# Attention and gated unit on one core: earlier first row maxima, and shorter GpSimd batches ahead of the routing pieces

## The chip, the core and the metric

The kernel runs on one core of a Trainium2 chip. The metric is the device time of one execution in microseconds (us). Before the change it is 1684.03 us, the median of three runs (1683.86, 1684.03 and 1685.21). Differences of under about 0.2% (3.4 us) are small beside what such runs tell apart; the text takes that as its bound for "no change".

The engines are named as in the profile: PE is TensorE (matmuls), PEld its weight loads, DVE is VectorE, ACT is ScalarE, POOL is GpSimd, SP is SyncE, which only issues DMAs here.

## The reference

Input x is 2048 tokens by 512. All arithmetic is in fp32.

```python
def _A_ref(x, wqkv, wo):                      # H = 32 heads, Dh = 16
    q, k, v = ...                             # x @ wqkv, split into heads
    p = softmax(einsum("bhqd,bhkd->bhqk", q, k) * Dh ** -0.5)
    return einsum("bhqk,bhkd->bhqd", p, v) ... @ wo

def _B_ref(x, w_gate, w_up, w_down):          # F = 1792
    return einsum("bsf,fd->bsd", sigmoid(x @ w_gate) * (x @ w_up), w_down)

g = sigmoid((x * gate_w).sum(-1, keepdims=True))
return g * _A_ref(x, ...) + (1 - g) * _B_ref(x, ...)
```

The sum `(x * gate_w).sum(-1)`, one number for each token, is what the text calls the routing logit.

## The kernel before

Every fp32 operand of the projections is held as a high and a low part (`xh`, `xl`), and a product is three matmuls (high by high, high by low, low by high). The softmax subtracts a row maximum, which has to be known before the exponentials of that row are made. So the scores are computed twice: once for the maxima (`sm_step`, line 292: a matmul into a PSUM bank, then a DVE reduction over it, line 294), and once, later and transposed, for the exponentials (`st_part`, line 679 and 681).

PE is used as two halves. A matmul with 64 rows or fewer takes the lower or the upper half of the array, and two such matmuls run side by side. Where a product has 128 rows, class `Sum` issues it as two halves, LOW and UP (line 162). Two Sums go together, one with its LOW halves while the other has its UP halves; then they change sides. The change of sides goes through a token: `turn` puts a no-operation on POOL that waits for the last matmul of the side, and the next half on PE waits for that no-operation (line 173 in the trace's lines). POOL's program is in order, so the token has its place behind the POOL work that was recorded ahead of it.

The order on PE, DVE, ACT and POOL is as the program records it. The order of the DMAs on SP is not written by hand; a scheduler places them.

The stages that the change touches are two.

**The value tiles.** After the first projections there are eight steps, t = 0, 2, ..., 14. In each, two Sums of 12 products (v for two blocks of 128 tokens) give 24 places, 12 for side LOW and 12 for side UP, each with one half of each Sum. Into these places go the first row maxima of the first pair of heads: 44 calls of `first_max`. One call is two matmuls into two of the four banks sm0 to sm3, one on each half of PE, and two DVE reductions. The tables `FIRST` and `EARLIEST` (the latter for t = 0) say at which place (side, 0 to 11) how many calls stand. A bank can be written again only when its reduction has read it. The maxima read `qs` and `ks`, which a DMA brings from DRAM.

**The periods.** Then come 256 periods, k = 0 to 255, each recorded by the string `STEADY`: eight maxima matmuls (m), eight score matmuls (t) and twelve dense halves (d) of a Sum that the generator `filling` hands out, one Sum a period, with the turn in the middle; then `values(k)`, sixteen short matmuls (line 842). The Sums of kind "side" come four to a job. Their weights are combined and split into high and low parts on POOL ("op", "hi", "lo" below: lines 448, 139 and 136), from two tiles that DMAs load.

POOL's work waits in queues (`later`, then `turnover`, then `slow`). `work(length)` takes steps from them until their estimated costs reach the length, and is called with 2.0 after the turn and with 2.6 at the period's end. When a job's last Sum is done, all steps of the next job's weights that are still in `turnover` are recorded at once (`while end in turnover`), at the end of that period, ahead of the next period's token.

In periods 75 to 122 six periods make a group, r = (k - 75) % 6. At r = 0 and 3 a DMA loads a tile "sq" (`split_load`), at r = 1 and 4 POOL splits it (`split_sum`, a cast and a subtraction), at r = 1 a DMA loads two blocks of x (`logit_load`), and at r = 3 and 4 DVE makes one block's logits each (`logits`: the multiplication with a sum, line 829). The tiles sq and x share two buffers, so some loads of sq wait for the second logits. Every eighth period DVE also ends a half of the maxima (lines 298 and 300, "mpad" and "mt"); its instructions stand at the start of the periods with k % 8 = 5.

Of the kernel before, what the change touches and what calls it, by code (L numbers as in the profile page):

```python
# [42 lines left out]
LOW, UP = 0, 1  # L43
# [3 lines left out]
def gated_mix(ctx, tc, x, xT, wqk, wv, wo, w_gate, w_up, w_down, gate_w, out):  # L47
# [8 lines left out]
    def turns(tiles):  # L56
        turn = iter(range(1 << 30))
        return lambda: tiles[next(turn) % len(tiles)]
# [112 lines left out]
    def turn(*runs):  # L171

        token = pool.nop()
        tc.add_manual_dep(token.ins, runs[-1].last.ins.name, SYNC, reason=SHARED)
        for r in runs:
            r.token = token
# [5 lines left out]
    def work(length):  # L182
        length -= over[0]
        while length > 0.3 and (later or turnover or slow):
            cost, step = (later or turnover or slow).pop(0)
            step()
            length -= cost
        over[0] = max(0.0, -length)
# [52 lines left out]
    def load_pair(p, cols=slice(0, S)):  # L241
        for t, src in enumerate((q_d, k_d)):
            for b in range(2):
                rows, r = slice((2 * p + b) * DH, (2 * p + b + 1) * DH), 64 * b
                to = (QS, KS)[t][p % 2]
                if t == 0:
                    two, one = src[:, rows, cols].rearrange("a d s -> d a s"), src[0, rows, cols]
                else:
                    two, one = src[0, rows, cols].unsqueeze(1), src[1, rows, cols]
                    two = two.to_broadcast([DH, 2, cols.stop - cols.start])  # L250
                sp.dma_start(to[r:r + 2 * DH, cols].bitcast(F32), two)
                sp.dma_start(to[r + 2 * DH:r + KM, cols].bitcast(F32), one)
# [50 lines left out]
    def put_max(half):  # L303

        p, i = half
        mt = mrow.pop(half)
        hl = keep.tile([P, 2, 32], F32R, name=f"mhl{p}_{i}", tag="mhl", bufs=2)

        def low():
            pool.tensor_tensor(hl[:, 1, :], mt, hl[:, 0, :].bitcast(F32), ALU.subtract)  # L310
            d = max_d[2 * p + i]
            sp.dma_start(d.rearrange("k r a j -> (k r) a j"), hl.bitcast(F32))
            for b in (1, 0):
                for a in range(2):
                    r = 64 * b + 3 * DH + a
                    rows_in[p, i] = sp.dma_start(QS[p % 2][r:r + 1, i * 1024:(i + 1) * 1024].rearrange(
                        "o (t k j) -> o t k j", t=8, k=4).bitcast(F32),
                        d[:, 8 * b:8 * b + 8, a, :].rearrange("k t j -> t k j").unsqueeze(0))
        return [(1.6, lambda: pool.tensor_copy(hl[:, 0, :], mt)), (0.25, low)]  # L319
# [293 lines left out]
    def first_max():  # L613
        if first:
            j, i = first.pop(0)
            one = sm_step(j)
            one(0, i)
            one(1, i)
# [36 lines left out]
    def tokens(t):  # L655
        return [((xh[:, k, t * P:(t + 1) * P], xl[:, k, t * P:(t + 1) * P]), w_v[k]) for k in range(KT)]

    def put_v(t, o, engine):
        to = v[:, t, :].rearrange("p (h c) -> p h c", c=VW)[:, :, :DH]
        o = o.rearrange("p (h c) -> p h c", c=DH)  # L660
        if engine is act:
            act.activation(to, o, AF.Copy)  # L662
        else:
            engine.tensor_copy(to, o)
# [3 lines left out]
    def st_part(k, b):  # L668

        p, r = divmod(2 * k, 32)  # L670
        i, kt = divmod(r, 16)
        qs, ks = QS[p % 2], KS[p % 2]
        r = 64 * b
        pt = ptile[k, b] = mid(f"p{k}_{b}")
        for a in range(2):
            for c in range(2):
                o = bank()
                q0 = i * 1024 + c * 512
                pe.matmul(o, ks[r:r + KR, (kt + a) * P:(kt + a + 1) * P], qs[r:r + KR, q0:q0 + 512],  # L679
                          start=True, stop=True)  # L680
                act.activation(pt[:, 2 * a + c, :], o, AF.Exp, scale=DH ** -0.5)  # L681
                yield

    FIRST = {(LOW, 2): 1, (LOW, 7): 1, (UP, 0): 2, (UP, 5): 1, (UP, 9): 1}
    EARLIEST = {(LOW, 10): 1, (UP, 0): 1, (UP, 4): 1, (UP, 9): 1}
    bank = turns([dn, banks[0]])
    ahead = st_part(0, 1)
    for t in range(0, NS, 2):
        two = [Sum(bankv(), tokens(t + a)) for a in range(2)]
        for g in (LOW, UP):  # L690
            for m in range(3 * KT):
                for _ in range((FIRST if t else EARLIEST).get((g, m), 0)):
                    first_max()
                two[0].half(g)
                two[1].half(1 - g)
                if (0, 0) in mrow and m == 2:
                    for _, step in put_max((0, 0)):
                        step()
                if t == NS - 2 and (g, m) in ((LOW, 11), (UP, 2), (UP, 5), (UP, 8)):
                    next(ahead)  # L700
                if t >= 12 and m == 6 and g == UP:
                    work(2.6)
            if g == LOW:
                turn(*two)
        if t < NS - 2:
            for a in range(2):
                put_v(t + a, two[a].o, act)
# [98 lines left out]
    def split_load(r):  # L806
        f, t, c = r // 8, r // 4 % 2, r % 4
        e = split_in[r] = keep.tile([P, 2, 512], F32R, name=f"sq{r}", tag="ev", bufs=2)
        sp.dma_start(e[:, 0, :].bitcast(F32), s_d[t, f, :, c * 512:(c + 1) * 512])

    def split_sum(r):
        f, t, c = r // 8, r // 4 % 2, r % 4
        e = split_in.pop(r)

        def store():
            for a in range(2):
                sp.dma_start((q_d, k_d)[t][a, (2 + f) * P:(3 + f) * P, c * 512:(c + 1) * 512],
                             e[:, 1 - a, :].bitcast(F32))
        split_later(e[:, 1, :], e[:, 0, :], e[:, 0, :].bitcast(F32), store)
# [3 lines left out]
    def logit_load(t):  # L823
        tok[t] = keep.tile([P, 2, D], F32, name=f"xn{t}", tag="ev", bufs=2)
        sp.dma_start(tok[t], x[t * P:(t + 2) * P, :].rearrange("(t p) d -> p t d", p=P))

    def logits(t, a):
        xn = tok[t][:, a, :]
        dve.tensor_tensor_reduce(xn, xn, gwb, scale=1.0, scalar=0.0, op0=ALU.mult, op1=ALU.add,
                                 accum_out=logit[:, t + a:t + a + 1])  # L830

    sums = {}

    def values(k):
# [67 lines left out]
    for k in range(NPER):  # L902
        n = 2 * k
        if n + LEAD == NSTEP:
            bank = bank7
            leave = dve.tensor_copy
        if 75 <= k < 123:
            t, r = divmod(k - 75, 6)
            if r in (0, 3):
                split_load(2 * t + r // 3)  # L910
            if r in (1, 4):
                split_sum(2 * t + r // 3)
            if r == 1:
                logit_load(2 * t)
            if r in (3, 4):
                logits(2 * t, r - 3)
        if n % 32 == 0 and n // 32 + 1 < NPAIR:
            load_pair(n // 32 + 1)
        parts["t0"], parts["t1"] = st_part(k, 0), st_part(k + 1, 1) if k + 1 < NPER else iter(())
        emit(STEADY if k < FREE else LAST, **parts)  # L920
        if run and run.done():
            run = next(fill, None)
        elif run and run.n:
            turn(run)
        for half in list(mrow):
            later[:0] = put_max(half)
        work(2.6)
        later.extend(soon)
        soon.clear()
        if k == NPER - 1:  # L930
            break
        if NPER - 16 < k <= NPER - 12:
            for _ in range(2):
                next(next(exps))
        spot[:] = [seven[SUMS]]
        values(k)
        if k == NPER - 17:
            loaded.extend(hidden_load(*chunks[m]) for m in range(2))
            early = [hidden_early(m) for m in range(2)]
            exps = iter([early[0]] * 4 + [early[1]] * 4)  # L940
        if 192 <= k < 215 and k % 8 != 4:
            next(dens[0], None)
        if k == NPER - 6:
            next(dens[1])
        if k == NPER - 2:
            raws = [late_raw(*late[m][:2]) for m in range(2)]
        if k == NPER - 13:
            early = chain(*early)
        if k >= NPER - 13:
            for _ in range(1 if k < FREE else 3):  # L950
                next(early, None)
# [137 lines left out]
```

## Time and profile before

| | |
|---|---|
| median of three runs | 1684.03 us |
| the profiled execution | 1684.2 us, of which the span from the first to the last instruction is 1682.4 us |
| PE busy in the span | 1677.3 us (100%) |
| DVE, ACT, POOL busy | 1451.8 us (86%), 1362.8 us (81%), 941.9 us (56%) |
| granted clock of TensorE | 1.000 |
| the value tiles | from 27.8 to 85.75 us |
| the periods 75 to 122 | about 503 to 771 us |

A row of the timeline gives the start in us, the duration in us, the engine, the line of the kernel, the operation, output<-inputs, the shapes and a count; in square brackets stands the time for which the engine had been idle before, and what ended that. Rows "SPq" are DMAs as SP issues them. PE's matmuls are pipelined, so that a duration of 0.39 us there does not mean that the next one waits so long. In a table by windows there stand, for a stretch, its length and each engine's busy time and instructions. Since PE is busy nearly all the time, the share of busy time tells little; what can be seen is whether the distance from one matmul to the next is longer than it is elsewhere.

### The profile page before, as it was taken

How to read it: one execution, taken by the hardware profiler on the slowest of the kernel's cores; microseconds unless marked ns; L12 is line 12 of the kernel's file. 1: busy time of each engine (PE TensorE's matmuls, PEld its weight loads, DVE VectorE, ACT ScalarE, POOL GpSimd, SP SyncE). 2: the span in 40 equal slices, each digit the busy share in tenths (PEclk: the TensorE clock that was granted, in tenths of full speed). 3: DMA queues.
4: the chain of work that ended last, by engine and by line, in shares of the span. 5: the costliest groups of instructions: out<-in, count | busy, mean ns of one | idle time of the engine just before them, and what ended most of it. 6: DMA issues, size and time to landing. Idle time of an engine off the chain costs nothing.

```text
span 1682.4 us, 34644 instructions
## 1 busy us (share of the span) xinstructions
PE 1677.3 (100%) x12485; PEld 1063.3 (63%) x12485; DVE 1451.8 (86%) x2347; ACT 1362.8 (81%) x2659; POOL 941.9 (56%) x922
## 2 busy tenths in 40 slices
PE   9999999999999999999999999999999999999999
PEld 7766566665656565656565666656565656568887
DVE  7988888888889999999888888888999888887853
ACT  4188898989888898889898989898898989983431
POOL 1034476547666666666666767676766667653110
PEclk9999999999999999999999999999999999999999
DMA  7511457356565564566635353534353534368861
GB/s 247 140 48 59 128 175 210 134 164 209 143 199 133 167 153 157 159 165 184 166 102 146 102 145 108 134 103 133 107 137 104 133 115 153 128 205 277 294 211 70
DMA packets 143788, 254.20 MB, mean 151 GB/s; under 512 B 24256, under 2 KB 36544, under 8 KB 140736
## 3 DMA queue, kind: packets, MB, share of 16 engines
q1 hardware_dynamic: 136000, 237.30, 47.1%
q10 hardware_dynamic: 7616, 14.68, 2.8%
q8 instruction: 98, 1.61, 0.4%
q14 instruction: 74, 0.61, 0.2%
HBM read 149.42 MB, written 102.50 MB: 150 GB/s over the span
## 4 chain that ended last, share of the span: by engine, by line
PE 97%; DVE 3%; issue 0%; DVEq 0%
PE dn L162 29%; PE sm L842 27%; PE sm L292 15%; PE sm L1034 5%; PE st L679 5%; PE sm L679 4%; PE st L292 2%; DVE stat L294 2%; PE dn L1034 2%; PE st L1034 2%; PE st L643 1%; PE st L149 1%; PE sm L149 1%; PE st L162 1%; PE st L842 1%; PE st L85 0%
## 5 line engine op out<-in xcount | busy, mean ns | idle before, releaser
L294 DVE TENSOR_REDUCE stat<-sm 128x1 f32<-128x512 f32 x1313 | 847.9, 681 | 140.4 <-PE sm L679 126.5
L681 ACT ACTIVATE p<-st 128x512 f32<-128x512 f32 x1019 | 619.2, 655 | 1.1 <-PE st L679 1.1
L681 ACT ACTIVATE p<-sm 128x512 f32<-128x512 f32 x1027 | 611.1, 632 | 0.5 <-PE sm L679 0.2
L292 PE MATMUL sm<-ks,qs 48*128 48x512 f32 x1313 | 522.6, 436 | 0.3
L842 PE MATMUL sm<-p,v 128*17 128x512 f32 x4016 | 480.0, 595 | 0.0
L294 DVE TENSOR_REDUCE stat<-st 128x1 f32<-128x512 f32 x735 | 479.5, 680 | 0.1
L679 PE MATMUL sm<-qs,ks 64*128 64x512 f32 x1027 | 427.6, 419 | 0.0
L679 PE MATMUL st<-qs,ks 64*128 64x512 f32 x1019 | 426.5, 419 | 0.0
L292 PEld LDWEIGHTS sm<-ks,qs 48*128 48x128 f32 x1313 | 239.6, 184 | 259.3 <-DVE stat L294 212.3
L859 POOL TENSOR_TENSOR sum<-sum,part 128x512 f32<-128x512 f32 x224 | 288.6, 1288 | 135.7 <-PE sm L679 118.4
L292 PE MATMUL st<-ks,qs 48*128 48x512 f32 x735 | 290.5, 395 | 0.0
L842 PEld LDWEIGHTS sm<-p,v 128*17 128x17 f32 x4016 | 93.2, 97 | 224.2 <-issue 155.1
L847 ACT ACTIVATE part<-sm 128x512 f32<-128x512 f32 x214 | 128.2, 599 | 124.4 <-issue 83.8
L542 POOL TENSOR_TENSOR chain<-chain,chain 128x512 f32<-128x512 f32 x96 | 124.1, 1292 | 156.3 <-PE sm L679 139.5
L679 PEld LDWEIGHTS st<-qs,ks 64*128 64x128 f32 x1019 | 187.7, 184 | 30.0 <-issue 3.4
L679 PEld LDWEIGHTS sm<-qs,ks 64*128 64x128 f32 x1027 | 189.6, 185 | 9.9 <-issue 5.1
L542 POOL TENSOR_TENSOR had<-chain,had 128x512 f32<-128x512 f32 x96 | 123.5, 1287 | 39.3 <-PE sm L679 20.3
L292 PEld LDWEIGHTS st<-ks,qs 48*128 48x128 f32 x735 | 137.3, 187 | 2.1 <-ACT v L662 0.3
L607 ACT ACTIVATE chain<-dn 128x512 f32<-128x512 f32 x128 | 89.2, 697 | 0.0
L542 POOL TENSOR_TENSOR side<-side,side 128x512 f32<-128x512 f32 x32 | 41.3, 1292 | 76.5 <-PE sm L679 66.1
L104 POOL TENSOR_TENSOR ol<-ot,oh 128x512 fp32r<-128x512 f32 (+1 forms) x8 | 14.7, 1840 | 102.5 <-ACT oh L101 102.5
L319 POOL CAST mhl<-mt 128x32 fp32r<-128x32 f32 x32 | 7.5, 236 | 102.7 <-DVE mt L300 102.7
(913 smaller groups left out, 3253.5 us busy)
## 6 DMA issues: line engine op xcount, KB each, us to landing
gul<-gu_d SPq DMA_DIRECT2D x56, 512.0 KB
had<-gu_d SPq DMA_DIRECT2D x84, 256.0 KB
gu_d<-had SPq DMA_DIRECT2D x84, 256.0 KB
gu_d<-side SPq DMA_DIRECT2D x56, 256.0 KB
pv_d<-sum SPq DMA_DIRECT2D x32, 256.0 KB
qs<-q_d SPq DMA_DIRECT2D x30, 256.0 KB
ks<-k_d SPq DMA_DIRECT2D x30, 256.0 KB
gu_d<-far SPq DMA_DIRECT2D x28, 256.0 KB
```

The costliest lines, as they stand in the source:

```text
L149: pe.matmul(o, a, b, start=(i == 0), stop=(i == len(ops) - 1))
L162: mm = pe.matmul(self.o, a[rows], b[rows], start=(self.n == 0), stop=(self.n == 2 * len(self.ops) - 1))
L292: pe.matmul(t, qs[r:r + KM, qt * P:(qt + 1) * P], ks[r:r + KM, g * 512:(g + 1) * 512], start=True, stop=True)
L294: dve.tensor_reduce(stat[half][:, b, qt % 8, g:g + 1], t, axis=AX.X, op=ALU.max)
L542: pool.tensor_tensor(to, u, w, ALU.add)
L607: leave = lambda e, o: act.activation(e, o, AF.Copy)
L679: pe.matmul(o, ks[r:r + KR, (kt + a) * P:(kt + a + 1) * P], qs[r:r + KR, q0:q0 + 512], start=True, stop=True)
L681: act.activation(pt[:, 2 * a + c, :], o, AF.Exp, scale=DH ** -0.5)
L842: pe.matmul(o[32 * c:32 * c + VW, :], v[:, 2 * k % 16 + a, h * VW:(h + 1) * VW], pts[c // 2][:, 2 * a + c % 2, :], start=(a == 0), stop=(a ...
L847: act.activation(e, o, AF.Copy)
L859: pool.tensor_tensor(s, s, e, ALU.add)
L1034: pe.matmul(down[t], a, b, start=(f == 0 and m == 0), stop=(f == NF - 2 and m == 5))
```

## The change

Three things change; what is computed stays the same.

First, the tables of the value tiles. At t = 0 there are now seven calls of `first_max` (from place LOW 1 on) where there were four (from LOW 10 on). At t = 2 and 4 there are six as before, one of them now at UP 10. From t = 6 on there are five in place of six. The last step, t = 14, has five in place of the four that were left over. The two calls in a row at the turn (UP 0) stay, and the call ahead of them moves from LOW 7 to LOW 8.

Second, the length of POOL's batch at the end of a period is 1.4 in place of 2.6 where the next period has logits.

Third, of the 16 logits pieces two, those of periods 85 and 109, are given in periods 86 and 110.

```diff
-    FIRST = {(LOW, 2): 1, (LOW, 7): 1, (UP, 0): 2, (UP, 5): 1, (UP, 9): 1}
-    EARLIEST = {(LOW, 10): 1, (UP, 0): 1, (UP, 4): 1, (UP, 9): 1}
+    FIRST = {(LOW, 3): 1, (LOW, 8): 1, (UP, 0): 2, (UP, 6): 1}
+    EARLIEST = {(LOW, 1): 1, (LOW, 4): 1, (LOW, 8): 1, (UP, 0): 2, (UP, 5): 1, (UP, 9): 1}
...
-                for _ in range((FIRST if t else EARLIEST).get((g, m), 0)):
+                for _ in range((FIRST if t else EARLIEST).get((g, m), 0) + (t in (2, 4) and (g, m) == (UP, 10))):
                     first_max()
...
+    def logits_at(k):
+        if not 75 <= k < 123:
+            return 0
+        r = (k - 75) % 6
+        return (r == 3) + 2 * (r == 4 and k % 8 != 5 or r == 5 and k % 8 == 6)
...
-            if r in (3, 4):
-                logits(2 * t, r - 3)
+            if logits_at(k):
+                logits(2 * t, logits_at(k) - 1)
...
-        work(2.6)
+        work(1.4 if logits_at(k + 1) else 2.6)
```

**PE at a turn of the value tiles.** The rows are PE's matmuls of step t = 6, from the last call ahead of the turn on. The lines 292 are a call's two matmuls (sm_69 to sm_72 are the four banks), the lines 162 are halves of the step's two Sums (st_66 and st_67). Before:

```order
L292 MATMUL sm_71<-ks_101,qs_100 128x512
L292 MATMUL sm_72<-ks_101,qs_100 128x512
L162 MATMUL st_66<-wv_l,xh 128x512
L162 MATMUL st_67<-wv_l,xh 128x512
L162 MATMUL st_66<-wv_h,xl 128x512
L162 MATMUL st_67<-wv_h,xl 128x512
L162 MATMUL st_66<-wv_h,xh 128x512
L162 MATMUL st_67<-wv_h,xh 128x512
L162 MATMUL st_66<-wv_l,xh 128x512
L162 MATMUL st_67<-wv_l,xh 128x512
L162 MATMUL st_66<-wv_h,xl 128x512
L162 MATMUL st_67<-wv_h,xl 128x512
```

Ten halves stand between this call and the turn's two calls, which come next. The same place now:

```order
L292 MATMUL sm_69<-ks_101,qs_100 128x512
L292 MATMUL sm_70<-ks_101,qs_100 128x512
L162 MATMUL st_66<-wv_h,xl 128x512
L162 MATMUL st_67<-wv_h,xl 128x512
L162 MATMUL st_66<-wv_h,xh 128x512
L162 MATMUL st_67<-wv_h,xh 128x512
L162 MATMUL st_66<-wv_l,xh 128x512
L162 MATMUL st_67<-wv_l,xh 128x512
L162 MATMUL st_66<-wv_h,xl 128x512
L162 MATMUL st_67<-wv_h,xl 128x512
L292 MATMUL sm_71<-ks_101,qs_100 128x512
L292 MATMUL sm_72<-ks_101,qs_100 128x512
```

Eight halves stand between this call and the first of the turn's two calls, which is the last two rows here. The turn's second call follows at once, on the banks that the first two rows of this fence write.

**POOL in the periods 77 to 79.** The rows are POOL's operations from the end of period 77 on. side_8r and side_1r are the raw weight tiles that DMAs load, side(0, 1)h and side(0, 1)l the high and low parts of the next job's weights (two blocks of each, one after the other), sq is the tile of `split_sum`; the lines 542 and 859 (865 now) are additions of the side Sums and of the value sums. Before:

```order
L448 TENSOR_TENSOR side_8r<-side_8r 128x256
L139 CAST side(0, 1)h<-side_8r 128x256
L136 TENSOR_TENSOR side(0, 1)l<-side_8r,side(0, 1)h 128x256
L542 TENSOR_TENSOR side_01_6288<-side_01_6288,side_00_6213 128x512
L859 TENSOR_TENSOR sum_1_5965<-sum_1_5965,part_6302 128x512
L448 TENSOR_TENSOR side_8r<-side_8r,side_1r 128x256
L448 TENSOR_TENSOR side_1r<-side_1r,side_8r 128x256
L139 CAST side(0, 1)h<-side_1r 128x256
L859 TENSOR_TENSOR sum_1_5965<-sum_1_5965,part_6371 128x512
L139 CAST sq_6304<-sq_6304 128x512
L136 TENSOR_TENSOR side(0, 1)l<-side_1r,side(0, 1)h 128x256
L136 TENSOR_TENSOR sq_6304<-sq_6304 128x512
```

Here the first three rows belong to the end of period 77, the two lines 448 and the cast after them to the end of 78, and only the last two rows to the end of 79. Now:

```order
L542 TENSOR_TENSOR side_01_6288<-side_01_6288,side_00_6213 128x512
L865 TENSOR_TENSOR sum_1_5965<-sum_1_5965,part_6299 128x512
L448 TENSOR_TENSOR side_8r<-side_8r 128x256
L865 TENSOR_TENSOR sum_1_5965<-sum_1_5965,part_6366 128x512
L139 CAST sq_6301<-sq_6301 128x512
L139 CAST side(0, 1)h<-side_8r 128x256
L136 TENSOR_TENSOR side(0, 1)l<-side_8r,side(0, 1)h 128x256
L448 TENSOR_TENSOR side_8r<-side_8r,side_1r 128x256
L448 TENSOR_TENSOR side_1r<-side_1r,side_8r 128x256
L139 CAST side(0, 1)h<-side_1r 128x256
L136 TENSOR_TENSOR side(0, 1)l<-side_1r,side(0, 1)h 128x256
L136 TENSOR_TENSOR sq_6301<-sq_6301 128x512
```

The seven rows from the cast "side(0, 1)h<-side_8r" on now all belong to the end of period 79, and so stand between the cast of sq and the token of period 80's turn. At the end of period 103 the same seven stand in place of the same two.

**DVE from the end of period 84 on.** The first two rows end a half of the maxima, the lines 829 are the second logits of the group (written as two instructions here, one in the trace), and the lines 294 are the reductions of the next maxima. Before:

```order
L298 TENSOR_REDUCE mpad_94<-stat_1_6236 128x16
L300 STREAM_TRANSPOSE mt_1_6769<-mpad_94 128x32
L829 ISA xn_6585,logit<-xn_6585,gwb 128x512
L829 ISA logit 128x1
L294 TENSOR_REDUCE stat_0_6798<-sm_72 128x1
```

Now:

```order
L298 TENSOR_REDUCE mpad_94<-stat_1_6236 128x16
L300 STREAM_TRANSPOSE mt_1_6769<-mpad_94 128x32
L294 TENSOR_REDUCE stat_0_6797<-sm_72 128x1
L294 TENSOR_REDUCE stat_0_6797<-st_65 128x1
L294 TENSOR_REDUCE stat_0_6797<-st_67 128x1
```

The logits follow now after the eighth of these reductions, one period later. At 109 it is the same.

## The prediction

> **What bounds the kernel now.** The page comes first, with the busy times and the shares of the chain of waits:
>
> ```profile
> PE 1677.3 (100%) x12485; PEld 1063.3 (63%) x12485; DVE 1451.8 (86%) x2347; ACT 1362.8 (81%) x2659; POOL 941.9 (56%) x922
> PE 97%; DVE 3%; issue 0%; DVEq 0%
> ```
>
> PE is the bound, and the change takes no matmul from it and adds none. So it can only move the gaps between matmuls. I read those in two places: the value tiles, where the first maxima move, and the periods 75 to 122. For the value tiles, this is the table by windows, one row a step from t = 0 to 14 (behind the busy time of each engine stand its instructions):
>
> ```profile
> core 0: us, PE busy (x) PEld busy (x) DVE busy (x) ACT busy (x) POOL busy (x), PEclk, DMA share, GB/s
> 27.80:34.55 6.75, 6.75 (x57) 5.36 (x58) 4.58 (x8) 0.60 (x1) 0.00 (x0) 1.00 0.97 242
> 34.55:41.55 7.00, 7.00 (x61) 5.46 (x59) 6.80 (x12) 1.09 (x2) 0.00 (x0) 1.00 0.51 155
> 41.55:48.90 7.35, 7.25 (x63) 6.09 (x61) 7.35 (x13) 1.08 (x2) 0.00 (x0) 1.00 1.03 253
> 48.90:56.05 7.15, 7.15 (x62) 5.69 (x60) 7.15 (x13) 1.08 (x2) 0.00 (x0) 1.00 1.06 217
> 56.05:63.25 7.20, 7.20 (x62) 5.65 (x60) 7.20 (x13) 1.08 (x2) 0.00 (x0) 1.00 0.98 313
> 63.25:70.45 7.20, 7.20 (x64) 5.78 (x62) 7.06 (x14) 1.09 (x2) 0.30 (x2) 1.00 0.06 24
> 70.45:78.20 7.75, 7.65 (x64) 5.87 (x62) 7.75 (x14) 1.09 (x2) 2.61 (x4) 1.00 0.09 24
> 78.20:85.75 7.55, 7.55 (x65) 6.25 (x61) 6.22 (x11) 3.38 (x6) 1.29 (x1) 1.00 0.07 19
> ```
>
> From t = 2 to t = 12 DVE is busy for the whole step: twelve reductions fill about 7.2 us. PE's gaps sit where it asks for a bank that DVE has not read yet. The timeline of the turn of t = 4:
>
> ```profile
> 44.33 0.39 PE L162 MATMUL st<-wv_h,xh 64*128 64x512 f32 x1
> 44.56 0.39 PE L162 MATMUL st<-wv_l,xh 64*128 64x512 f32 x1
> ...
> 45.53 0.18 PEld L292 LDWEIGHTS sm<-ks,qs 48*128 48x128 f32 x1 [0.41 <-DVE stat L294]
> 45.54 0.50 PE L162 MATMUL st<-wv_h,xh 64*128 64x512 f32 x1
> 45.87 0.40 PE L162 MATMUL dn<-wv_h,xh 64*128 64x512 f32 x1
> ```
>
> Two halves that run side by side, or the two matmuls of a call, take one slot: 44.56 - 44.33 = 0.23 us. After a wait for a bank (0.41 here) one more slot is longer, 45.87 - 45.54 = 0.33, so a wait costs 0.10 on top.
>
> How long a call holds its banks shows at a call that DVE meets idle, in the timeline of t = 2 (three reductions in one row, two of them this call's):
>
> ```profile
> 36.05 2.06 DVE L294 TENSOR_REDUCE stat<-sm 128x1 f32<-128x512 f32 x3
> 36.40 0.40 PE L292 MATMUL sm<-ks,qs 48*128 48x512 f32 x2
> ```
>
> The matmuls start at 36.40 and the second reduction ends at 36.05 + 2.06 = 38.11: 1.71 us. I estimate that 0.06 more pass until PE starts again; with it the wait of 0.16 below fits t = 6 (7.15, less thirty slots of 0.23 and 0.10, is 0.15).
>
> **The value tiles.** There are 44 calls and 192 pairs of halves before and after, so the slots sum to the same; the waits decide. The turn has two calls in a row. The first finds two free banks, the second needs those of the call ahead of the turn. That call stood 7 slots (five pairs and two calls) ahead, 7 x 0.23 = 1.61, and was to be waited for 1.77 - 1.61 = 0.16 even with DVE idle. From LOW 8 it stands 6 slots ahead, 1.38, and the wait is 0.39, with the restart 0.49, at every turn. Step by step:
>
> t = 0: three more calls are 3 x 0.23 = 0.69, and its turn, where one call found its banks free, now waits 0.49: +1.18, to 7.93. t = 2: thirty slots (24 pairs, six calls) are 6.90, and with 0.49 that is 7.39 where 7.00 stood: +0.39. t = 4: 7.39 for 7.35: +0.04. t = 6, 8 and 10: 29 slots and 0.49 are 7.16 for 7.15, 7.20 and 7.20: -0.07 together. The call taken away there gives its slot back, but the longer wait takes all of it. t = 12: 7.16 for 7.75, since the half's end on DVE, which lies ahead of this step before, now falls beside the turn of t = 10, behind reductions that PE does not wait for: -0.59. t = 14: a fifth call, 0.23, and a longer wait, of which I take 0.07: +0.3. The sum is **+1.25**.
>
> The first call now comes one slot into t = 0, at 28.05. Its last input was issued here:
>
> ```profile
> 24.84 0.58 SPq L252 DMA_DIRECT2D ks<-k_d  x1
> ...
> 527.60 0.32 SPq L809 DMA_DIRECT2D sq<-s_d  x1
> ...
> 531.11 0.61 POOL L139 CAST sq<-sq 128x512 fp32r<-128x512 f32 x1 [0.64 <-DMA sq<-s_d]
> 531.68 0.73 POOL L136 TENSOR_TENSOR side(0, 1)l<-side_1r,side(0, 1)h 128x256 fp32r<-128x256 f32 x1
> 532.37 1.28 POOL L136 TENSOR_TENSOR sq<-sq 128x512 fp32r<-128x512 f32 x1
> ```
>
> The nearest load whose end is seen, sq, came 531.11 - 527.92 = 3.19 after its issue; by that ks would land at 28.61 and the call would wait 0.56. It is a smaller load, so I take 0, and keep 0 to +0.6. Below nothing a later landing cannot go.
>
> **The logits.** The same kind of table for the periods 78, 79, 85, 102 and 109:
>
> ```profile
> 519.29:525.29 6.00, 5.95 (x46) 3.27 (x44) 6.00 (x11) 5.22 (x11) 5.48 (x7) 1.00 0.31 93
> 525.29:530.86 5.57, 5.57 (x45) 3.36 (x44) 5.47 (x11) 4.90 (x11) 4.48 (x5) 1.00 0.35 107
> 558.73:564.61 5.88, 5.88 (x47) 3.33 (x45) 5.81 (x13) 5.22 (x11) 3.52 (x5) 1.00 0.41 128
> 653.82:659.70 5.88, 5.88 (x46) 3.26 (x45) 5.88 (x11) 5.20 (x11) 5.37 (x7) 1.00 0.31 93
> 693.14:699.01 5.87, 5.87 (x46) 3.28 (x44) 5.80 (x13) 5.21 (x11) 3.52 (x5) 1.00 0.40 127
> ```
>
> Period 79, with logits, takes 5.57 like any other. In 78 and 102 DVE is full, and in 85 and 109 it has two instructions more. The timelines of 78 and 85 say why:
>
> ```profile
> 520.90 1.27 DVE L829 CUSTOM_DVE_ANT_0 xn<-xn,gwb 128x512 f32<-128x512 f32 x1
> 520.90 0.73 POOL L448 TENSOR_TENSOR side_8r<-side_8r 128x256 f32<-128x256 f32 x1
> ...
> 560.45 0.22 DVE L298 TENSOR_REDUCE mpad<-stat 128x16 f32<-128x64 f32 x1
> ```
>
> The logits started together with a POOL operation over a raw weight and took 1.27; in period 79 DVE's whole sum is 0.53 lower. The end of a half (0.22 for its first part) stands in 85 and 109. After the change that POOL operation is later in 78 and 102, and 86 and 110 hold the logits without the half's end. Each of the four then takes 5.57: 0.43 + 0.31 + 0.31 + 0.30 = **-1.35**. The cover of the moved logits is DVE's 0.10 of slack in a period like 79.
>
> **The batch.** The limit only delays POOL's work, and PE feels that where it waits for a token or for weights. The order shows two such places, the ends of 79 and 103, where seven operations now stand behind the cast of sq. That cast waits for sq until 531.11, and the logits that free sq's buffer have not moved. Then, with durations of rows above, 0.61 cast, 0.40 "h" (row below), 0.73 "l", two operations of 0.73, 0.40 "h", and five gaps of about 0.08: 531.11 + 0.61 + 0.40 + 0.73 + 0.73 + 0.73 + 0.40 + 0.40 = 535.1, where "l" begins. PE's turn:
>
> ```profile
> 534.70 0.18 PEld L162 LDWEIGHTS dn<-xh,side(0, 1)h 64*128 64x128 f32 x1
> ...
> 666.87 0.33 SPq L108 DMA_DIRECT2D side_11r<-in_w_up_dram  x1
> ...
> 672.74 0.74 POOL L448 TENSOR_TENSOR side_11r<-side_11r 128x256 f32<-128x256 f32 x1 [0.95 <-DMA side_11r<-in_w_up_dram]
> 673.54 0.40 POOL L139 CAST side(1, 4)h<-side_11r 128x256 fp32r<-128x256 f32 x1
> ...
> 674.68 0.18 PEld L162 LDWEIGHTS dn<-xh,side(0, 4)h 64*128 64x128 f32 x1
> 674.72 0.73 POOL L448 TENSOR_TENSOR side_11r<-side_11r,side_4r 128x256 f32<-128x256 f32 x1
> ```
>
> When the token passes is seen at period 105: PE loads for the second side at 674.68, and the operation that POOL starts at 674.72 stands ahead of that token in POOL's program. So the token does not wait for all of POOL's work ahead of it to end; it passes about when the last operation or two are still to come. By this the token of period 80 comes at about 535.1, against 534.70: 0.4 and 0.1 of restart, **+0.5**, and as much at 104. If two operations may be pending, nothing is lost; if none, 0.73 + 1.28 = 2.0 more is. I take +0.5, as 674.68 and 674.72 are the nearest rows, and keep 0 and 2.5.
>
> [...]
>
> One more link: the raw tile is loaded again only when the last "l" has read it, some 3.5 us later than before (535.9 for 532.4). side_11r needed 672.74 - 666.87 = 5.87 from issue to use, with 1.94 more from there to the token (674.68). At 105 and 81 the next token then comes late: by nothing if the transfer is quick, as the DMA queue is emptier by then, and by 2.9 if it is as slow again (666.87 + 3.45 + 5.87 + 1.94 = 678.1 against 674.68 + 0.5). I take +0.6 at 105, where the load was already waited for, and +0.3 at 81: **+0.9**, with 0 and 5.8 as ends. The weights' first halves in 80 and 104 still come about 0.3 ahead of PE; that is their cover.
>
> **The sum.** 1.25 - 1.35 + 2 x 0.5 + 0.9 = +1.8 on the profiled execution's 1684.2, which lies 0.17 above the median; against the median 1684.03 that is **1685.8 us**, +0.11%. About 0.2% is what a measurement of this kernel tells from no change.
>
> **The rivals.** *Nothing new waits in the periods*: tokens pass earlier and the reload is quick. Then 1684.03 + 1.25 - 1.35 = 1683.9. The tight start of 672.74 speaks against it. For it speaks what the list of who waited for the token has of PE in the whole trace, 0.3 us, once:
>
> ```profile
>   PEld dn L162: 0.3, 1
> ```
>
> *The token waits for the whole batch*: 2.5 in place of 0.5 at 80 and at 104, so 1685.8 + 4.0 = 1689.8, slower. 674.68 speaks against it. It decides as soon as the wait exceeds 1.3 at each.
>
> *The reload comes late*, by 2.9 at 81 and at 105: 1685.8 + 5.8 - 0.9 = 1690.7; at 105 alone 1688.1. The 5.87 us speak for it, the emptier queue against.
>
> *DVE is never late in the value tiles.* Seven calls in t = 0 and five from t = 6 on take DVE out of saturation. If the call of LOW 8 freed its banks in 1.38 us in place of 1.77, no turn would wait. The waits of before, by the table and slots of 0.23 (0.10, 0.45, 0.25, 0.30, 0.30, 0.85 in t = 2 to 12), 2.25 in all, would go: 1684.03 - 2.25 - 1.35 = 1680.4, faster, if nothing new waits in the periods. The 1.71 us, measured with an idle DVE, speak against it.
>
> **How the numbers follow.** My forecast of waits as computed, with ends from 1684.5 to 1687.4, has 0.55; nothing new in the periods 0.15; both are within 0.2%, 0.70. The token waiting for the batch has 0.12, the late reload 0.10, other waits 0.03: slower 0.25. DVE never late has 0.05: faster 0.05. The low end is 1682.1: no new waits in the periods, -1.35, and the value tiles shorter by 0.6 (t = 12 alone). The high end is 1689.8, the token's rival. Outside lie DVE never late and the late reload at both places, some 0.15 with what I have not thought of.
>
> **What would show it.** Right: steps of about 7.9, 7.4, 7.4 and then 7.2 in the value tiles, each with a wait for DVE of about 0.4 at the turn's second call; 5.57 in periods 78, 85, 86, 102, 109 and 110; half a microsecond more in 80 and 104, less than one in 81 and 105. Wrong: steps under 7.0 from t = 6 on; 6 or more in period 86; a POOL token as releaser of PE for 2 us or more; or another period over 5.6.

## The result and the profile after

The changed kernel takes 1686.5 us (median of 22 runs, 1685.23 to 1687.96), the kernel before 1684.14 us (22 runs beside them). The ratio is 1.0013, with a 95% interval of 1.0007 to 1.0018: 0.13% slower, within what the text counts as no change by its bound of 0.2%, but outside the interval of no effect. The forecast was 1685.8.

The page of the changed kernel shows the same bound as before, PE busy for all of a span that is 1.6 us longer:

```profile
span 1684.0 us, 34647 instructions
PE 1678.0 (100%) x12485; PEld 1064.6 (63%) x12485; DVE 1452.6 (86%) x2347; ACT 1363.1 (81%) x2659; POOL 938.8 (56%) x922
```

The table by windows of the value tiles, one row a step, t = 0 to 14, from the first half of one step to the first half of the next (the last row ends with the last half):

```profile
27.09:35.52 8.43, 8.22 (x63) 6.48 (x64) 7.70 (x13) 0.60 (x1) 0.00 (x0) 1.00 0.86 229
35.52:42.74 7.22, 7.21 (x64) 5.81 (x61) 7.22 (x13) 1.09 (x2) 0.00 (x0) 1.00 0.64 194
42.74:49.97 7.23, 7.22 (x63) 5.86 (x61) 7.23 (x13) 1.09 (x2) 0.00 (x0) 1.00 1.08 261
49.97:56.96 6.99, 6.99 (x62) 5.72 (x59) 6.99 (x13) 1.09 (x2) 0.00 (x0) 1.00 1.02 207
56.96:63.92 6.96, 6.96 (x61) 5.96 (x58) 6.14 (x11) 1.09 (x2) 0.00 (x0) 1.00 0.80 301
63.92:70.92 7.00, 6.99 (x61) 5.63 (x59) 6.05 (x12) 1.09 (x2) 0.46 (x2) 1.00 0.01 2
70.92:77.92 7.00, 7.00 (x62) 6.15 (x59) 6.71 (x12) 1.09 (x2) 2.45 (x3) 1.00 0.06 9
77.92:85.57 7.65, 7.65 (x64) 6.68 (x61) 6.65 (x11) 3.14 (x6) 1.28 (x1) 1.00 0.10 33
```

They start 0.72 us earlier than before (27.09 against 27.81), for a reason that has nothing to do with the change (last section), and end only 0.06 later. Their length is what compares: 58.48 us now, and 57.70 before, from 27.81 to 85.51 in the same way. That is **+0.78**. Step t = 0 alone is 1.68 longer, and t = 14 is 0.33 longer (7.65 for the 7.33 from 78.18 to 85.51); t = 6, 8 and 10 are some 0.2 shorter each, and t = 12 is 0.75 shorter.

The same view for periods 78, 80, 81, 83, 85 and 102:

```profile
519.57:525.14 5.57, 5.57 (x46) 3.36 (x44) 5.48 (x11) 5.00 (x11) 3.24 (x4) 1.00 0.32 98
530.71:536.52 5.81, 5.81 (x47) 3.39 (x45) 5.12 (x9) 5.25 (x11) 5.13 (x8) 1.00 0.58 129
536.52:542.60 6.08, 6.03 (x46) 3.25 (x45) 5.15 (x10) 5.09 (x11) 5.50 (x8) 1.00 1.04 204
548.16:555.07 6.91, 6.04 (x47) 3.27 (x45) 5.69 (x10) 5.31 (x12) 3.17 (x4) 1.00 0.94 316
560.63:566.20 5.57, 5.57 (x46) 3.41 (x45) 5.32 (x11) 5.01 (x11) 3.07 (x5) 1.00 0.33 121
655.41:660.98 5.57, 5.57 (x46) 3.37 (x44) 5.49 (x11) 5.01 (x11) 3.14 (x4) 1.00 0.33 98
```

And 80, 81 and 83 in the kernel before:

```profile
530.86:536.45 5.59, 5.59 (x47) 3.38 (x45) 4.89 (x9) 5.03 (x11) 4.16 (x5) 1.00 1.01 241
536.45:542.01 5.56, 5.56 (x46) 3.34 (x45) 4.86 (x9) 5.03 (x11) 4.96 (x8) 1.00 1.09 188
547.58:553.16 5.58, 5.58 (x46) 3.36 (x45) 4.89 (x9) 5.01 (x11) 4.14 (x4) 1.00 0.91 280
```

The four logits periods take 5.57 to 5.59 (109 is the 5.59): -1.33 in all. But 80, 81 and 83 took 5.59, 5.56 and 5.58 before, so they cost 0.22, 0.52 and 1.33 more. Periods 104 and 105 take 5.57 and 5.58, as before.

Where PE waits in 83 is said by the list of waits of 546 to 556 us (time in all, times, longest):

```profile
POOL sq L139 <- DMA sq<-s_d: 3.7, 1, 3.7
PEld dn L162 <- POOLq L173: 1.3, 1, 1.3
```

PE waits 1.3 us for the token, and the token stands behind the cast of sq, for which POOL waits 3.7 us. SP's timeline tells why sq is late; the last row is the same load in the kernel before:

```profile
535.66 0.33 SPq L108 DMA_DIRECT2D side_8r<-in_w_up_dram  x1
536.05 1.18 SPq L817 DMA_DIRECT2D q_d<-sq  x2
537.32 0.58 SPq L251 DMA_DIRECT2D qs<-q_d  x1
...
541.86 0.30 SPq L252 DMA_DIRECT2D ks<-k_d  x1
...
547.18 0.32 SPq L809 DMA_DIRECT2D sq<-s_d  x1
...
543.35 0.32 SPq L809 DMA_DIRECT2D sq<-s_d  x1
```

From this reload to the load of sq SP's rows have the same order in both traces. The reload of side_8r, 3.2 us later than before (535.66 for 532.44), stands ahead of the stores of q_d, of the loads of the next pair's qs and ks, and of the load of sq. What held the issue of sq at last is named by the chain of waits of 540 to 556 us in the changed kernel:

```profile
538.58 8.58 DMA qs<-q_d
...
547.18 5.43 DMA sq<-s_d
```

The load of the pair's qs, eight issues ahead of the load of sq, was in flight for 8.6 us, and the load of sq was issued when it had landed, 3.8 us later than before.

A last piece is small and far away: the periods that begin with the value matmuls numbered 147, 157, 176, 186 and 215 are 0.09, 0.21, 0.08, 0.21 and 0.21 us longer than before, and 243 is 0.09 shorter, +0.71 in all. (The expectations below name these periods, and 67, by that number, one less than the period's; 80, 81 and 83 are counted as in the prediction.) So the profile's sum is 0.78 - 1.33 + 0.22 + 0.52 + 1.33 + 0.71 = 2.23, and 2.23 - 0.72 for the early start is the 1.5 by which its last value matmuls come later (1498.38 against 1496.84). The medians differ by 2.4, close to the sum without the early start.

### The profile page after: what moved, and what is told of

The parts are those of the page before. It is cut to its first block, busy times and chain, and to the rows that moved or that the text cites. A ratio compares the mean times of both kernels' runs of the same rounds, so it can differ in the third digit from the quotient of the medians.

```text
span 1684.0 us, 34647 instructions
## 1 busy us (share of the span) xinstructions
PE 1678.0 (100%) x12485; PEld 1064.6 (63%) x12485; DVE 1452.6 (86%) x2347; ACT 1363.1 (81%) x2659; POOL 938.8 (56%) x922
## 3 DMA queue, kind: packets, MB, share of 16 engines
q8 instruction: 98, 1.61, 0.4%
## 4 chain that ended last, share of the span: by engine, by line
PE 98%; DMA 1%; DVE 1%; POOL 0%; issue 0%; SPq 0%; ACT 0%; POOLq 0%
PE dn L162 30%; PE sm L848 27%; PE sm L292 15%; PE sm L1040 5%; PE st L679 4%; PE sm L679 4%; PE dn L1040 2%; PE st L292 2%; PE st L162 2%; PE st L1040 2%; PE st L643 1%; PE st L149 1%; PE sm L149 1%; PE st L848 1%; DMA sq<-s_d 1%; DMA qs<-q_d 1%
```

## The experiments

Each kernel was timed in five rounds beside the kernel before, whose median was 1683.95 in the first four, 1684.4 in the next four and 1684.19 in the last two. One comparison resolves about 0.09% (1.5 us), so most readings below rest on the profiles, which place the time to some 0.05 us.

**The tables alone** (`FIRST`, `EARLIEST` and the call at UP 10, on the kernel before).

```diff
-    FIRST = {(LOW, 2): 1, (LOW, 7): 1, (UP, 0): 2, (UP, 5): 1, (UP, 9): 1}
+    FIRST = {(LOW, 3): 1, (LOW, 8): 1, (UP, 0): 2, (UP, 6): 1}
...
```

> Only the tables of the value tiles are changed (FIRST, EARLIEST and the call at UP 10); POOL's batches and the logits stay as before. Theory: as the trace after the change shows it, the value tiles end 0.06 us later than before, so the time is that of before, 1684.1 to 1684.4. Rival (the prediction's arithmetic, a longer wait at every turn): +1.25, 1685.4. Of the small longer periods that only the trace after the change shows (36, 71, 147, 157, 176, 186 and 215, together 0.9 us): if they come from the earlier maxima they stand here at the same places, if they are accidents of one execution they stand elsewhere or not at all.

Measured: 1684.95, ratio 1.0005 (0.9996 to 1.0014). The value tiles take 58.49 us, step by step as in the changed kernel, and start at 27.75. So neither the 0.06 by which the tiles end later in the changed kernel's trace nor the prediction's 1.25 is the price: by the profile the tables cost 0.8, and the early start had hidden it. None of the small longer periods stands here; 67, which like 71 varies from one execution to the next, is 0.28 longer. Period 78 takes 5.57 in place of 6.00 although POOL's batch is as before. The timeline shows by how little:

```profile
521.89 0.68 DVE L829 CUSTOM_DVE_ANT_0 xn<-xn,gwb 128x512 f32<-128x512 f32 x1
521.88 1.29 POOL L448 TENSOR_TENSOR side_8r<-side_8r 128x256 f32<-128x256 f32 x1
```

Before, the same two started together (520.90) and DVE's took 1.27. Here they start 0.01 us apart, DVE's takes its 0.68 and POOL's takes 1.29. One of the two loses some 0.6 us, with starts 0.01 us apart or less, and the period is longer where it is DVE (6.00 before) and not where it is POOL (5.57 here).

**The limit alone** (logits stay in 85 and 109).

```diff
-        work(2.6)
+        work(1.4 if 75 <= k + 1 < 123 and (k + 1 - 75) % 6 in (3, 4) else 2.6)
```

> Only POOL's batch is limited to 1.4 at the end of a period ahead of logits; the logits stay in 85 and 109, the tables stay. Theory: periods 78 and 102 give back 0.43 and 0.31, periods 80, 81 and 83 take 0.23, 0.52 and 1.32 more, so +1.3: about 1685.5. Rival: the wait in period 83 belongs to something else in the change (the moved logits, or the earlier maxima): then 83 takes 5.58 and the time is 1684.1 or a little less.

Measured: 1685.81, ratio 1.0012 (1.0003 to 1.0021), as the theory has it. 78 and 102 give back 0.43 and 0.31; 80 and 81 take 0.11 and 0.13 more. In the profiled execution, one of the two slowest of eleven (1688.2), 83 waited 2.0 us for the token, and period 84 took 7.26 besides. The windows of period 83 up to the end of its wait, and of the value matmuls behind it:

```profile
547.27:553.26 5.99, 4.46 (x35) 2.20 (x33) 5.29 (x9) 4.51 (x9) 1.58 (x3) 1.00 0.97 331
554.84:558.71 3.87, 3.87 (x21) 0.81 (x21) 1.58 (x4) 1.44 (x4) 0.91 (x1) 0.56 0.57 178
```

The granted clock fell to 0.56 for 3.87 us. The sixteen value matmuls, in one row of 1.91 us in the changed kernel (555.07), take 3.60 here (554.84), and 1.7 us is lost on top of the wait. The wait of 2.0 us and the slow stretch behind it cost 3.7 together. The small periods stand here too, at the same places.

**The moved logits alone.**

```diff
+    def logits_at(k):
...
-            if r in (3, 4):
-                logits(2 * t, r - 3)
+            if logits_at(k):
+                logits(2 * t, logits_at(k) - 1)
```

> Only the two logits of 85 and 109 are given in 86 and 110. Theory: 85 and 109 take 5.57 in place of 5.88, 86 and 110 stay at 5.57, nothing else moves: -0.6, about 1683.5. Rival: the later logits free the buffers of x and sq later and some load is late behind them: a period of 87 to 92 or 111 to 116 is longer, and the gain is gone.

Measured: 1684.2, ratio 1.0001 (0.9993 to 1.0010). 85 and 109 are 0.29 shorter each, but 86 and 110 are 0.35 and 0.33 longer. Neither theory had that: in 86 the logits meet a POOL operation over a weight, as in 78.

```profile
566.38 1.21 DVE L829 CUSTOM_DVE_ANT_0 xn<-xn,gwb 128x512 f32<-128x512 f32 x1
...
566.32 0.73 POOL L448 TENSOR_TENSOR side_9r<-side_9r 128x256 f32<-128x256 f32 x1
```

POOL's starts 0.06 earlier here, and DVE's takes long. The move alone only shifts the loss; it gains because the limit clears POOL out of 86.

**The changed kernel without the limit at the ends of 77 and 78.**

```diff
-        work(1.4 if logits_at(k + 1) else 2.6)
+        work(1.4 if logits_at(k + 1) and k not in (77, 78) else 2.6)
```

> The changed kernel without the limit at the ends of periods 77 and 78, so that POOL's work for the side weights is spread as before there; everything else as changed. Theory: the waits of 80, 81 and 83 (0.23 + 0.52 + 1.32) all come from the seven operations at the end of 79 and go together, and 78 has its 0.43 back: 2.07 - 0.43 = 1.64 below the changed kernel, about 1684.7, or 0.85 below before if the small longer periods are accidents: 1683.3. Rival: 83 waits for another reason (the sq load itself or the bus): then 83 keeps its 1.32, and the time is about 1685.9.

Measured: 1684.98, ratio 1.0005 (0.9996 to 1.0014). 80, 81 and 83 take 5.56 to 5.58, 78 has its 6.00 back, 85, 102 and 109 keep their gain, and the small periods stay. So without the seven operations at the end of 79 all three waits are gone.

**The pair's loads in period 82 in place of 80.**

```diff
-        if n % 32 == 0 and n // 32 + 1 < NPAIR:
+        if k % 16 == (2 if 80 <= k < 96 else 0) and n // 32 + 1 < NPAIR:
             load_pair(n // 32 + 1)
```

> The changed kernel, with the loads of the next pair's qs and ks, which period 80 issues, given in period 82. Theory: the wait of period 83 comes by way of SP, which issues in order: the late second side weight holds SP, the qs and ks loads behind it hold SP further, and the load of sq comes 3.8 us later than before. With those loads behind the load of sq, 83 takes 5.58 (1.32 less), while 80 (5.81) and 81 (6.08) stay as they are: about 1685.2. Rival: sq itself is late because the pair's bytes fill the DMA engines, or because its source is written late: then 83 stays near 6.9 and the time near 1686.5.

Measured: 1685.49, ratio 1.0006 (0.9997 to 1.0015). Period 83 of this kernel:

```profile
547.88:553.46 5.58, 5.58 (x47) 3.37 (x45) 4.88 (x9) 5.01 (x11) 4.07 (x4) 1.00 1.00 236
```

The wait is gone, with the side weight's reload as late as in the changed kernel (535.76). The load of sq now stands far ahead of that reload:

```profile
529.01 0.40 SPq L809 DMA_DIRECT2D sq<-s_d  x1
```

So the place of this load among SP's issues makes the wait. The run does not part the reload from the pair's loads, since the load of sq has passed both. From issue to cast the load took 5.72 us before (543.35 to 549.07) and 5.58 in the changed kernel (547.18 to 552.76), so it was late by its issue and not by a slower transfer of its own. 80 and 81 take 5.72 and 5.70, still longer than before.

**LOW 7 ahead of the turn**, on the changed kernel.

```diff
-    FIRST = {(LOW, 3): 1, (LOW, 8): 1, (UP, 0): 2, (UP, 6): 1}
+    FIRST = {(LOW, 3): 1, (LOW, 7): 1, (UP, 0): 2, (UP, 6): 1}
```

> The changed kernel, with the call ahead of the turn back at LOW 7 in place of LOW 8, at every step. Theory: the turn's second call asks for its banks 0.17 us too early in the steps t = 2 to 12, and each such wait costs 0.10 more; one slot (0.23) earlier they are free. Six steps of about 6.7 to 6.95 in place of 7.0 to 7.2, so the value tiles get 1.6 us shorter than with LOW 8 (58.48 from the first to the last of their halves) and about 0.8 shorter than before (57.70); the time about 1684.9. Rival: DVE is still the bound there, the wait only moves to the next call, and the value tiles stay at 58.5 and the time at 1686.5.

Measured: 1685.5, ratio 1.0005 (0.9997 to 1.0014). The value tiles take 57.76, 0.72 less than with LOW 8. That is half of what the theory said. The five-call steps fall from 7.0 to 6.8 (6.78, 6.86 and 6.77 at t = 8 to 12), but t = 0 stays at 8.44, the six-call steps at 7.19 and 7.15, and t = 6 at 6.96; from t = 2 to 6 DVE is busy for the whole step. There the rival is right.

**The limit only ahead of the first logits and the moved ones.**

```diff
-        work(1.4 if logits_at(k + 1) else 2.6)
+        work(1.4 if logits_at(k + 1) and k not in (78, 84, 90, 96, 102, 108, 114, 120) else 2.6)
```

> The changed kernel, with the limit only ahead of the first logits of a group and ahead of the two moved ones, not ahead of the second logits of the other groups (79, 91, 97, 103, 115, 121). Theory: at the end of 79 three weight operations and sq's low part are left behind the cast in place of seven operations, the token comes at about 533, and the weight's reload 1.3 us later than before in place of 3.5: 80, 81 and 83 take 5.6, and the four logits periods keep their 5.57. Against before: +0.8 in the value tiles, -1.33 in the logits, so 1683.6, and up to 0.7 more if the small longer periods (147 to 215) stay. Rival: the second logits need the limit, and 79 or 103 takes 5.9 or more.

Measured: 1684.14, ratio 0.9997 (0.9988 to 1.0006). Periods 80, 81 and 83 take 5.58, 5.57 and 5.57, the four logits periods keep their gain, and the small longer periods are gone. The last was not expected; it led to the run after the next.

**Other tables on top of that**: LOW 7, and six calls at t = 0 to 6.

```diff
-    FIRST = {(LOW, 3): 1, (LOW, 8): 1, (UP, 0): 2, (UP, 6): 1}
-    EARLIEST = {(LOW, 1): 1, (LOW, 4): 1, (LOW, 8): 1, (UP, 0): 2, (UP, 5): 1, (UP, 9): 1}
+    FIRST = {(LOW, 3): 1, (LOW, 7): 1, (UP, 0): 2, (UP, 6): 1}
+    EARLIEST = {(LOW, 2): 1, (LOW, 7): 1, (UP, 0): 2, (UP, 5): 1, (UP, 9): 1}
...
-... + (t in (2, 4) and (g, m) == (UP, 10))):
+... + (t in (2, 4, 6) and (g, m) == (UP, 10))):
```

> The narrow limit, the moved logits, and other tables: LOW 7 ahead of the turn, six calls at t = 0 (from LOW 2), 2, 4 and 6, and five from t = 8 on. Theory: no wait at the turns and no DVE backlog from t = 0, so that the value tiles end about 1 us earlier than before; with -1.33 from the logits and no new wait at 80, 81 and 83 the time is 1681.8 to 1682.5, below both kernels. Rival: the six calls of t = 2 to 6 saturate DVE as before, the value tiles stay at 57.7, and the time is 1682.8 to 1683.5.

Measured: **1682.31**, ratio 0.9988 (0.9979 to 0.9997): by its interval faster than the kernel before, by 0.12%, which is still inside the bound of 0.2%. The value tiles take 57.00, 0.70 less than before:

```profile
27.81:84.81 57.00, 57.00 (x477) 46.65 (x476) 54.35 (x91) 10.26 (x19) 4.22 (x6) 1.00 0.57 155
```

Steps 0 to 6 take 7.18 to 7.24, DVE's pace from t = 2 on; t = 8 to 12 take 6.77 to 6.93. Period 83 took 6.11 in this execution: the load of sq was issued at 543.61 and its cast began at 550.61, and PE waited 0.5 us for the token. With the same limit the run before this one has 543.12 and 549.50, and no wait. So the narrow limit leaves little room at 83; that it removes the wait is not shown.

**One more ACT instruction.** A small copy in period 126 of the changed kernel. In its trace ACT has 3628 records where the kernel before has 3629, one fewer ahead of period 130. Each kernel that shows the small longer periods has 3628 too, and each that doesn't has 3629. (The expectation counts the program's own, five fewer: 3623 and 3624.)

```diff
+        if k == 126:
+            act.activation(g1[:, :1], logit[:, :1], AF.Copy)
```

> The changed kernel with one more small ACT instruction, a copy of one column into a column that is written again later, at the start of period 126. The small longer periods 147, 157, 176, 186 and 215 (0.09, 0.21, 0.08, 0.21, 0.21) stand in every kernel whose ACT program has 3623 instructions, and in none of those with 3624; the one instruction is missing ahead of period 130, and the order behind it is the same. Theory: the place of ACT's instructions in its stream, not work, makes these periods longer: with 3624 instructions again, 147, 157, 176, 186 and 215 take 5.58 and the kernel is 0.7 us faster, about 1685.8 where it had 1686.5. Rival: they come from what the limit does to POOL's or SP's order: then they stay.

Measured: 1684.79, ratio 1.0007 (0.9998 to 1.0015). 147, 157, 176, 186 and 215 take what they take before, and 243 has its 0.09 back. The window that 157 begins, in the changed kernel and then in this one:

```profile
967.77:973.55 5.78, 5.78 (x46) 3.14 (x44) 5.08 (x9) 5.09 (x11) 2.73 (x3) 1.00 0.15 50
```

```profile
966.92:972.48 5.56, 5.56 (x46) 3.35 (x44) 4.86 (x9) 4.98 (x11) 2.52 (x3) 1.00 0.15 52
```

So the rival falls: the place of the instructions in ACT's stream decides whether these periods are longer. Period 83 took 6.20 here, 80 and 81 took 5.70.

**The best version with the pair's loads in 82.** The edit of the fifth run on the eighth.

> The narrow limit, the moved logits, the tables with LOW 7 and six calls at t = 0 to 6, and the pair's loads in period 82 in place of 80. Theory: as the run with the same tables and limit, 1682.3, less the 0.5 that period 83 took there in its profile (a wait for the token behind the cast of sq): 1681.8 to 1682.3. Rival: the wait in 83 was an accident of one execution, or the later loads of the pair make the scores of the next pair wait: 1682.3 or more.

Measured: 1683.21, ratio 0.9994 (0.9985 to 1.0003). 83 takes 5.58 in this profile, and the last value matmuls come 2.2 us earlier than before, but the end comes only 1.0 earlier. The 1.2 us lie behind the last matmul: from the start of DVE's last operation to the end of the span it is 5.1 us (1676.34 to 1681.4) where the kernel before has 3.9 (1678.54 to 1682.4). The fifth run, the other one with the loads in 82, has 5.1 as well (1678.63 to 1683.7), and no other run has. So this edit goes with 1.2 us more at the end of the program; the traces do not say why. By its time the kernel is not better than the eighth run, and a gain over the kernel before is not shown.

## Why the prediction came out as it did

The time lies inside the range, with the sign that was forecast and nearly the size (+1.8 forecast, +2.4 measured). But the terms held only in part, and their errors cancel: that the sum came so close is luck.

**The value tiles: +1.25 forecast, +0.78 measured.** By steps 7.93, 7.39, 7.39, 7.16 three times, 7.16 and 7.85 were forecast; 8.43, 7.22, 7.23, 6.99, 6.96, 7.00, 7.00 and 7.65 came. (The last forecast counts to 85.75; to the last half, as here, it is some 0.2 less, and held.) Two things failed. The first is the wait at the turn, put at 0.39. The turn of t = 2 of the changed kernel, from the call ahead of it on:

```profile
37.59 0.61 PE L292 MATMUL sm<-ks,qs 48*128 48x512 f32 x2
...
38.75 1.12 PE L292 MATMUL sm<-ks,qs 48*128 48x512 f32 x4
...
39.38 0.18 PEld L292 LDWEIGHTS sm<-ks,qs 48*128 48x128 f32 x1 [0.41 <-DVE stat L294]
39.39 0.73 PE L162 MATMUL st<-wv_h,xh 64*128 64x512 f32 x2
39.72 0.63 PE L162 MATMUL st<-wv_l,xh 64*128 64x512 f32 x2
```

The price of a call held: from its first matmul (37.59) to PE's restart (39.38) 1.79 us pass, and 1.77 to 1.80 at the turns of t = 2 to 12, where 1.77 was taken. The distance did not hold. The two matmuls of a call start together in the row of 36.40 (two in 0.40 us) but one slot apart here (two in 0.61), and the one that waits is the last of the four from 38.75 on. It stands seven slots behind the first matmul of the call ahead, 1.61, and not six, 1.38. So it starts 0.40 after the matmul before it, one slot and a wait of 0.17, and the restart costs the forecast 0.10. That takes some 0.2 off each of the six steps t = 2 to 12.

The second is t = 0, where I added slots and one wait. Its DVE rows:

```profile
27.82 0.69 DVE L228 TENSOR_TENSOR qe<-st,qe 128x512 fp32r<-128x512 f32 x1 [2.03 <-ACT qe L227]
28.43 7.86 DVE L294 TENSOR_REDUCE stat<-sm 128x1 f32<-128x512 f32 x13
```

The first call is made at 27.42, but DVE still has an operation of the projections to do, and its reductions start at 28.43. From there thirteen run without a gap, 0.60 each. Step 0 runs at DVE's pace with a late start, and the step is 0.50 longer than forecast. The price of a call at an idle DVE does not hold where calls come faster than DVE reads them. That PE would not wait for the load of ks, taken as 0, held.

**The logits: -1.35 forecast, -1.33 measured.** All four periods came as forecast. The collision of DVE and POOL that I read from the two rows at 520.90 is what the runs show again. Here are six places where the logits and a POOL operation of line 448 start within 0.1 us of each other, and in each one of the two takes 0.5 to 0.6 us longer:

| | DVE's logits (0.68 alone) | POOL's line 448 (0.73 alone) | POOL's start |
|---|---|---|---|
| before, 520.90 | 1.27 | 0.73 | at the same time |
| before, 526.89 | 0.67 | 1.25 | 0.03 behind |
| before, 655.41 | 1.18 | 0.73 | 0.10 ahead |
| before, 661.31 | 0.68 | 1.25 | 0.02 behind |
| the tables alone, 521.89 | 0.68 | 1.29 | 0.01 ahead |
| the moved logits, 566.38 | 1.21 | 0.73 | 0.06 ahead |

DVE lost where POOL's start was 0.06 or 0.10 ahead, POOL where its start was 0.02 or 0.03 behind; for starts as close as 0.01 the records do not tell which was first. What makes one of the two take longer the runs do not show.

**The token: 2 x 0.5 forecast, 0.22 and 0 measured.** The reading of when a token passes was right. POOL's rows ahead of the turn of 80:

```profile
534.42 0.40 POOL L139 CAST side(0, 1)h<-side_1r 128x256 fp32r<-128x256 f32 x1
534.90 0.74 POOL L136 TENSOR_TENSOR side(0, 1)l<-side_1r,side(0, 1)h 128x256 fp32r<-128x256 f32 x1
535.60 1.28 POOL L136 TENSOR_TENSOR sq<-sq 128x512 fp32r<-128x512 f32 x1
```

And the token itself, with who waited for it:

```profile
L173 POOLq EVENT_SEMAPHORE  x1: 17/17/17, 534.9 to 534.9; - x1
  PEld dn L162: 0.2, 1
```

It passes at 534.9, when "l" begins and the low part of sq has not, so the rival by which it waits for the whole batch fell; 535.1 was forecast. At 104 it passes at 670.3, just in time, because the cast of sq started with the period (666.55) and not 0.27 behind it, as before (665.54 against 665.27).

**The reload: +0.9 forecast, +0.52 measured.** At 81 POOL's first operation on the reloaded tile starts at 539.72 (537.34 before), and PE waits 0.5 us for the token (0.3 forecast). But only the last 0.36 us before 539.72 is a wait for the reload. Until then POOL was still busy with what the burst had pushed back, the low part of sq and two additions. In the four other profiles of kernels with the full limit POOL does not wait for the reload at all (it starts at 539.42 in the run of the pair's loads), and 81 takes only 0.13 to 0.14 more. So the forecast link shows in one execution of five, and POOL's own backlog, which had no term, in all. At 105 nothing was lost where 0.6 was forecast. The reload there was issued at 671.12, and POOL was busy up to 674.76 anyway.

**What had no term: +1.33 in 83 and +0.71 in the small periods.** The step that failed is the one more link: I followed the reload of the raw tile from SP to POOL and not to what stands behind it on SP itself. The order of SP's issues in the trace of before shows that the load of sq does (532.44 and 543.35). 80 has loads of a next pair (every sixteenth period), with the load of sq behind them; 104 has none, and there the load of sq is issued at 664.67, ahead of the reload. That is why 79's burst cost so much and 103's nothing, and the run with those loads in 82 agrees. The size of this wait varies with the execution: 1.33, 2.0 ahead of a fallen clock, 0.35 and 0.62 in four profiles of kernels with the full limit and the loads in place, and 0.5 in one of the two with the narrow limit. The small periods could not be read from the trace of before: that ACT's program gets one instruction shorter could have been counted, but not what that costs.

In sum, the tables cost 0.78, the burst at the end of 79 costs 2.07, the small periods cost 0.71, and the 1.33 gained in the four logits periods does not pay for them.

## What to carry to other kernels

When an operation is delayed on one engine, follow its results through the order of the DMA issues too: here what stood behind the delayed issue cost 1.33 us (the load of sq, in 83), the reload itself at most 0.52 (in 81). A limit that clears an engine ahead of one consumer moves the work to the next deadline (here the end of 79, for 2.07 us); look what is flushed there, and limit only where a collision was seen to cost something. And before a wait is worked out from a price and a count of slots, see which matmul of a call it is that waits and where that one starts: a grouped row hides whether two run together or one slot apart.

## What the runs showed of the hardware

**The fast clock begins at a varying time.** Early matmuls come 0.43 us apart, until the gap falls to 0.23. In the rows this is a pair of 1.05 us as late as 5.81 in the kernel before, and a pair of 0.63 at 5.67 in the changed kernel:

```profile
5.81 1.05 PE L643 MATMUL st<-xh,qk_0l 128*128 128x512 f32 x2
```

```profile
5.67 0.63 PE L643 MATMUL st<-xh,qk_0l 128*128 128x512 f32 x2
```

In this pair the whole 0.72 of the early start arises there: the tenth matmul behind the first starts at 5.39 before and 5.36 now, the fifteenth at 7.32 and 6.60. In the traces the record of the full clock begins at 7.06 and 5.52, beside the first gaps under 0.3 us (7.08 and 5.67). Over the profiles that first gap lies between 3.96 and 7.08 us, and the value tiles start between 27.09 and 27.88. The two do not go together throughout: the gap falls first, at 3.96, in the run without the limit at 77 and 78, and its tiles start at 27.70, so something else varies too. That is up to 0.8 us that varies while the program up to there is the same, and it can hide an effect of the same size in one pair of traces.

**A fallen clock behind a wait of 2 us.** PE's wait of 2.0 us in the run of the limit alone was followed, 1.6 us after its end, by a granted clock of 0.56 for 3.9 us; behind the wait of 1.3 us in the changed kernel it stayed at 1.00. Such a fall came once; whether the wait set it off was not tried.

**One instruction more or less on ACT makes or removes small stalls elsewhere.** In the three periods that are 0.21 longer, one ACT operation starts 0.72 us after the one ahead of it (969.79 and 970.51 in the changed kernel) in place of 0.50 (968.75 and 969.25 before), and no releaser is named:

```profile
969.79 0.60 ACT L853 ACTIVATE part<-sm 128x512 f32<-128x512 f32 x1 [0.57 <-issue]
970.51 0.60 ACT L681 ACTIVATE p<-sm 128x512 f32<-128x512 f32 x1
```

The places are 29 periods apart (157, 186, 215, and 147, 176), and one instruction added ahead of them removes all five. What stalls ACT at these places the runs do not show.
